# Three more unread 128-column products at the start, in place of 33 small ones

## The chip, the cores and the metric

One core of a Trainium2 chip runs the whole kernel. The metric is the device time of one execution in microseconds (us); lower is better. The kernel before takes 313.28 us (median of 3 runs, 313.25 to 313.35). TensorE is called PE here (its weight loads PEld), VectorE DVE, ScalarE ACT, GpSimd POOL, and SyncE, which issues the data transfers, SP.

## What is computed

The inputs are q, k and v (4 batches, 4 heads, 1088 positions, 32 features), two small projections S1 and S2 (8 by 32), and the weights of a gated layer. With `phi(x)` the outer product of `x @ S1.T` and `x @ S2.T` (64 features), the first part is linear attention:

```python
kv = sum over s of phi(k)[s] v[s];  z = sum over s of phi(k)[s]
x  = (phi(q) @ kv) / (phi(q) @ z + 1e-06)          # heads side by side: (4, 1088, 128)
```

The second part, per batch:

```python
h = relu(x @ w_in); u, v = h[..., :512], h[..., 512:]
v_n = (v - mean(v)) / sqrt(var(v) + 1e-06)
v_s = w_spatial @ v_n + b_spatial[:, None]
out = (u * v_s) @ w_out
```

## The kernel before

The long products are made in three passes over operands that are split into a high and a low half (`wTh`/`wTl`/`wl`, `vh`/`vl`, `xh`/`xl`, lines 1172 to 1183 and 1417 for the positions, 606 to 608 for the others). Work goes batch by batch. A batch begins with its attention: `project` (line 781) makes the two projections of keys or queries, ACT copies one of them (`ka`, line 786), DVE multiplies them out into the features (`kp`, line 788), and `part` (line 818) sums features times values into `kv`. Line 818 is a burst of very short PE instructions: products of 32 features by 33 columns, four of them side by side, 72 products for a batch. PE makes a product of full 32-bit floats in two passes, and each pass is one weight load and one matmul in the trace, so the 72 products are 144 loads and 144 matmuls. In batch 0 the burst comes in three parts (`kv0:1` to `kv0:3`, with 24 products each), in the other batches in one (`kv1`, `kv2`, `kv3`).

The order of the work is written out by hand: `SEQ` lists every operation by name and engine (`kab00:1@PE` is the first projection of the keys of batch 0), and each engine runs its own entries in that order. `Order.schedule` replays the list with planned costs to choose buffers and the order in which the instructions are written down. It also puts unread filler products (`Fill`, line 638, 128 columns) before a PE operation where its plan leaves PE room, up to the time `FILL_TO`. In batch 0 PE's list is: the warm-up `wps:1` to `wps:7`, `kab00`, `kab01`, `kab02`, `kv0:1`, `qab00`, `kv0:2`, `kv0:3`, `tq00`, `tq01` (transposes of the query features, line 863), `qab01`, `qab02`, `nd00` (line 877), and so on to `xt0` (line 891).

The warm-up is work that nobody reads. DVE fills a tile `z9` (lines 622 and 623); `wps:1` is the function `small`, which makes 33 products of 32 columns, spread over the four quarters of the array, and `wps:2` to `wps:7` are one product of 128 by 128 columns each (line 633). All write the same bank. The first real work of PE, `kab00`, needs the projection weights `sk`, which DVE prepares, and the first tile of keys, which SP loads.

Of the kernel before, what the change touches and what calls it, by code (L numbers as in the profile page):

```python
# [35 lines left out]

EXP_LO = 2.0 ** -15
EXP_HI = 122879.9921875
N_SMALL, N_WARM = 33, 6


PS_BUFS = {"po": 3, "sp": 2, "pu": 1, "sd": 2}
# [17 lines left out]
AFTER_W = (7.0, 13.0, 13.0)  # L60

SEQ = """
s_raw:1@SP z9:1@DVE z9:2@DVE wi_raw1:1@SP eps:1@ACT v92:1@POOL wps:1@PE v90:1@POOL kt00:1@SP v91:1@POOL wz:1@POOL kt01:1@SP wps:2@PE kt02:1@SP
wps:3@PE v93:1@POOL v00:1@SP wps:4@PE sk:1@DVE mask_sb:1@SP wps:5@PE sk:2@DVE sk:3@DVE qt00:1@SP wps:6@PE sk:4@DVE sk:5@DVE wps:7@PE v01:1@SP sk:6@DVE
sk:7@DVE b32:1@SP wi_x1:1@DVE v02:1@SP wi_x1:2@DVE kab00:1@PE ident_sb:1@SP wi_x1:3@DVE qt01:1@SP kab01:1@PE ka00:1@ACT qt02:1@SP kp00:1@DVE
ka01:1@ACT eps:2@DVE kp01:1@DVE kab02:1@PE kv0:1@PE ka02:1@ACT wi_raw0:1@SP qab00:1@PE kp02:1@DVE wt30:1@SP qa00:1@ACT wt10:1@SP qp00:1@DVE kv0:2@PE
wt80:1@SP kv0:3@PE wi_x1:4@DVE tq00:1@PE tq01:1@PE kd0:1@DVE qpT00:1@ACT wi_x1:5@DVE qab01:1@PE qpT01:1@ACT wi_x1:6@DVE qab02:1@PE qa01:1@ACT
nd00:1@PE qp01:1@DVE wi_x1:7@POOL qa02:1@ACT wi_x0:1@ACT wt01:1@SP qp02:1@DVE wt11:1@SP tq10:1@PE wt50:1@SP tq11:1@PE rec0:1@DVE qpT10:1@ACT wt00:1@SP
rec0:2@DVE tq20:1@PE wih:1@ACT x320:1@DVE wt20:1@SP wi_x0:2@DVE bh:1@ACT qpT11:1@ACT xt0:1@PE wt21:1@SP wil:1@DVE tq21:1@PE xh0:1@ACT wTl:10@SP
nd01:1@PE wi_x0:3@DVE wt40:1@SP xl0:1@DVE wTh:10@ACT wt31:1@SP wTh:9@ACT wi_x0:4@DVE pv000:1@PE wt41:1@SP qpT20:1@ACT rec1:1@DVE qpT21:1@ACT wt51:1@SP  # L70
# [247 lines left out]
class Order:  # L318
# [12 lines left out]
    def op(self, eng, cost, fn, r=(), w=(), kb=0, alts=(), sh=False, after=0.0, f4=False, name=None):  # L331
        o = Op()
        o.n, o.eng, o.fn, o.kb, o.f4 = len(self.ops), eng, fn, kb, f4
        o.alts = ((eng, cost, fn), *alts)
        name = name or next(((x[0] if isinstance(x, tuple) else x).name for x in w), "out")
        self.named[name] = self.named.get(name, 0) + 1
        o.name = f"{name}:{self.named[name]}"
        o.sh, o.after, o.behind = sh, after * 1e3, None
        deps = {}
        r, w = ([(t, key) for t0, key in (x if isinstance(x, tuple) else (x, None) for x in xs) for t in (t0.tiles if isinstance(t0, Whole) else [t0])] for xs in (r, w))  # L340

        def split(x):
            return x if isinstance(x, tuple) else (x, None)

        def touching(table, t, key):
            for (t2, k2), v in table.get(t, {}).items():
                if key is None or k2 is None or k2 == key:
                    yield (t2, k2), v

        for x in r:  # L350
            t, key = split(x)
            for _, d in touching(self.last_w, t, key):
                deps[d] = True
        for x in w:
            t, key = split(x)
            for _, d in touching(self.last_w, t, key):
                deps[d] = True
            for _, ds in touching(self.readers, t, key):
                for d in ds:
                    deps[d] = True  # L360
        for x in r:
            t, key = split(x)
            self.readers.setdefault(t, {}).setdefault((t, key), []).append(o)
        for x in w:
            t, key = split(x)
            for k, _ in list(touching(self.last_w, t, key)):
                if key is None or k[1] == key:
                    del self.last_w[t][k]
            for k, _ in list(touching(self.readers, t, key)):
                if key is None or k[1] == key:  # L370
                    del self.readers[t][k]
            self.last_w.setdefault(t, {})[t, key] = o
        deps.pop(o, None)
        o.deps, o.succ = list(deps), []
        for d in o.deps:
            d.succ.append(o)
        o.tiles = list(dict.fromkeys(split(x)[0] for x in (*r, *w)))
        o.first = []
        for t in o.tiles:
            if t.tag is not None:  # L380
                o.first.append(t)
                t.users.append(o)
        self.ops.append(o)
        return o
# [148 lines left out]
def tile_kernel(ctx: ExitStack, tc: tile.TileContext, kT, qT, vA, sks, idn, msk, wT, w_in, w_out, bsp, out):  # L533
# [6 lines left out]
    nc = tc.nc  # L540
# [59 lines left out]
    op, tl = k.op, k.tile  # L600

    def bank(tag, name):
        return tl(tag, name, [P, 512])
# [17 lines left out]
    z9 = tl("u", "z9", [P, P])  # L621
# [1 line left out]
    op("DVE", 165, lambda: nc.vector.memset(z9[64:66], 1.0), w=[z9])  # L623

    wps = bank("sd", "wps")
    def small():
        for i in range(N_SMALL):
            q = 32 * (i % 4)
            nc.tensor.matmul(wps[q:q + 32, :32], z9[:, q:q + 32], z9[:, :32], start=True, stop=True, tile_position=(0, q))

    op("PE", 1100, f4=True, fn=small, r=[z9], w=[wps])
    for i in range(N_WARM):
        op("PE", 420, f4=True, fn=lambda: nc.tensor.matmul(wps[:, :P], z9.ap, z9.ap, start=True, stop=True), r=[z9], w=[wps])

# [7 lines left out]
    eps = tl(None, "eps", [P, 2])  # L642
# [57 lines left out]
    sk = tl(None, "sk", [P, 2 * NSK])  # L700
    s_raw = tl("pl", "s_raw", [P, 384])
# [8 lines left out]
    kd0 = tl("u", "kd0", [P, 2, 2, D + 1])  # L710
# [288 lines left out]
    def hidden_v(b, st, g):  # L999
# [39 lines left out]
        def small(out, in0, scalar, in1, op0, op1, r, w):  # L1039
            op("DVE", 163, lambda: v.scalar_tensor_tensor(out=out(), in0=in0(), scalar=scalar, in1=in1(), op0=op0, op1=op1), r=r, w=w, sh=True)  # L1040

        small(lambda: t1.ap, lambda: mv[:, :, 1], LN_EPS, lambda: rs.ap, ALU.add, ALU.mult, [rs, mv], [t1])
        small(lambda: t1.ap, lambda: t1.ap, -0.5, lambda: rs.ap, ALU.mult, ALU.mult, [rs], [t1])
        small(lambda: rs.ap, lambda: t1.ap, 1.5, lambda: rs.ap, ALU.add, ALU.mult, [t1], [rs])

# [592 lines left out]
```

## Time and profile before

| what | value |
|---|---|
| median of 3 runs | 313.28 us |
| the profiled execution, its own time | 313.46 us |
| its span on the core | 311.7 us |
| instructions in the span | 6906 |
| PE busy | 305.7 us (98%) |
| DVE, ACT, POOL busy | 221.0, 180.0, 94.3 us |

The span runs from the first to the last instruction of the program; 1.76 us of the profiled execution lie around it. All numbers of rows below come from that one execution, with times from the start of the span. A PE that is busy is not PE at its peak, since matmuls are pipelined and their ends are modelled. "issue" as the cause of a wait means that the engine waited for no semaphore that the profile shows.

### The profile page before, as it was taken

To read this page: it belongs to the slowest core of one execution; us is meant where nothing else is said; L and a number is where in the kernel's file an instruction comes from. 1 tells how busy PE (TensorE), PEld (TensorE's weight loads), DVE (VectorE), ACT (ScalarE), POOL (GpSimd) and SP (SyncE) were. 2 spreads that over 40 slices of the span, in tenths; PEclk is the share of its full clock that TensorE was granted. 3 is DMA by queue.
4 is the path that set the end of the run, shared out by engine and by line. 5 is a ranking of instruction groups with operands and counts; after the bars stand their busy time and mean duration, and the time that the engine had idled before them with its cause. 6 is when DMAs were issued, how large, how long until landed. Compare 5 with 4: busy or idle time off the path is not lost.

```text
span 311.7 us, 6906 instructions
## 1 busy us (share of the span) xinstructions
PE 305.7 (98%) x2588; PEld 294.7 (95%) x2588; DVE 221.0 (71%) x549; ACT 180.0 (58%) x428; POOL 94.3 (30%) x124
## 2 busy tenths in 40 slices
PE   7899999999999999999999999999999999999995
PEld 7788999999999999999999999999999999999995
DVE  6899977636666855473694478898976767978572
ACT  2499974525765553567564776897346345654430
POOL 2145015243311046652113654510110312152400
PEclk9999999999999999999999999999999999999999
DMA  7974147573300055710334864223000170410002
GB/s 243 311 219 161 28 139 207 180 210 103 86 1 23 3 155 158 214 52 0 124 90 141 294 214 117 87 64 84 25 0 2 35 299 0 144 47 0 2 0 72
DMA packets 22989, 33.78 MB, mean 108 GB/s; under 512 B 2988, under 2 KB 21420, under 8 KB 22956
## 3 DMA queue, kind: packets, MB, share of 16 engines
q1 hardware_dynamic: 22812, 33.21, 33.7%
q8 instruction: 20, 0.33, 0.5%
q10 hardware_dynamic: 144, 0.13, 0.1%
q14 instruction: 13, 0.11, 0.1%
HBM read 26.79 MB, written 6.54 MB: 107 GB/s over the span
## 4 chain that ended last, share of the span: by engine, by line
PE 96%; DVE 2%; issue 1%; ACT 0%; DVEq 0%; ACTq 0%
PE sp L1172 15%; PE sp L1174 13%; PE sp L1181 13%; PE sd L1417 9%; PE sp L1417 7%; PE sd L606 4%; PE sd L607 4%; PE sd L608 4%; PE pu L606 3%; PE po L606 3%; PE pu L608 3%; PE pu L607 3%; PE po L607 2%; PE po L608 2%; PE sp L1183 2%; PE sd L781 2%
## 5 line engine op out<-in xcount | busy, mean ns | idle before, releaser
L1172 PE MATMUL sp<-wTh,vh 128*128 128x332 f32 (+1 forms) x286 | 93.7, 329 | 0.0
L1174 PE MATMUL sp<-wTh,vl 128*128 128x332 f32 (+1 forms) x240 | 78.7, 328 | 0.0
L1172 PEld LDWEIGHTS sp<-wTh,vh 128*128 128x128 f32 x286 | 53.7, 188 | 0.5
L1174 PEld LDWEIGHTS sp<-wTh,vl 128*128 128x128 f32 x240 | 45.1, 188 | 0.2
L1181 PE MATMUL sp<-wl,vh 128*128 128x332 f32 x128 | 39.7, 310 | 0.0
L1181 PE MATMUL sp<-wTl,vh 128*128 128x424 f32 x112 | 38.0, 348 | 0.0
L614 DVE TENSOR_TENSOR g<-u,g 128x332 fp32r<-128x332 f32 (+1 forms) x41 | 24.6, 600 | 11.9 <-ACT g L693 6.2
L1165 ACT ACTIVATE u<-pu 128x332 f32<-128x332 f32 (+1 forms) x44 | 20.6, 467 | 19.5 <-PE pu L608 11.7
L1209 DVE TENSOR_TENSOR u<-sp,u 128x332 f32<-128x332 f32 (+1 forms) x43 | 22.3, 521 | 11.7 <-PE sp L1183 10.8
L1013 DVE BATCH_NORM_STATS2 st<-vt 128x6 f32<-128x512 f32 x36 | 24.3, 685 | 8.3 <-ACT vt L1011 8.1
L617 POOL TENSOR_TENSOR r<-pl,r 128x384 fp32r<-128x384 f32 (+1 forms) x18 | 17.8, 996 | 32.0 <-ACT r L693 13.7
L1011 ACT ACTIVATE vt<-sd 128x512 f32<-128x512 f32 x36 | 21.1, 601 | 11.0 <-PE sd L608 10.6
L693 ACT CAST g<-u 128x332 fp32r<-128x332 f32 (+1 forms) x41 | 20.0, 489 | 8.6 <-DVE u L1209 3.5
L950 POOL TENSOR_TENSOR pl<-pl,pl 128x384 f32<-128x384 f32 (+1 forms) x18 | 17.9, 1001 | 21.7 <-DMA pl<-qd 7.6
L1181 PEld LDWEIGHTS sp<-wl,vh 128*128 128x128 f32 x128 | 24.0, 188 | 0.0
L1085 ACT CAST vh<-vt 128x384 fp32r<-128x384 f32 x44 | 21.5, 509 | 1.8 <-DVE vt L1049 1.1
L1181 PEld LDWEIGHTS sp<-wTl,vh 128*128 128x128 f32 x112 | 21.0, 188 | 0.1
L1087 POOL TENSOR_TENSOR vl<-vt,vh 128x384 fp32r<-128x384 f32 (+1 forms) x16 | 14.6, 914 | 21.1 <-ACT vh L1085 16.9
L1052 ACT ACTIVATE vt<-vt,sm,sm 128x512 f32<-128x512 f32 x18 | 14.4, 814 | 3.5 <-DVE sm L1040 3.5
L986 DVE STREAM_TRANSPOSE sd<-c 128x384 f32<-128x384 f32 (+1 forms) x9 | 5.1, 568 | 15.9 <-ACT c L983 15.8
L606 PE MATMUL pu<-xh,wih 128*128 128x332 f32 (+1 forms) x48 | 16.0, 334 | 0.0
L1087 DVE TENSOR_TENSOR vl<-vt,vh 128x384 fp32r<-128x384 f32 (+1 forms) x28 | 14.3, 515 | 2.1 <-ACT vh L1085 2.0
(317 smaller groups left out, 805.4 us busy)
## 6 DMA issues: line engine op xcount, KB each, us to landing
pl<-in_wT SPq DMA_DIRECT2D x34, 166.0 KB
v<-in_vA SPq DMA_DIRECT2D x12, 198.0 KB
kt<-in_kT SPq DMA_DIRECT2D x12, 192.0 KB
pl<-qd SPq DMA_DIRECT2D x12, 192.0 KB
pl<-qd SPq DMA_DIRECT2D x24, 96.0 KB
vd<-vt SPq DMA_DIRECT2D x3, 768.0 KB
vt<-vd SPq DMA_DIRECT2D x3, 768.0 KB
c<-in_qT SPq DMA_DIRECT2D x9, 192.0 KB
```

The source lines that it names most:

```text
L606: nc.tensor.matmul(o, ah, bh, start=start, stop=False)
L607: nc.tensor.matmul(o, ah, bl, start=False, stop=False)
L608: nc.tensor.matmul(o, al, bh, start=False, stop=stop)
L614: return lambda: nc.vector.tensor_tensor(out=o(), in0=a(), in1=bb(), op=ALU.subtract)
L1013: op("DVE", 690, lambda stats=stats, t=t: nc.vector.bn_stats(out=stats.ap, in_=vt[:, t]), r=[(vt, t)], w=[stats])
L1085: op("ACT", c_act(384), lambda: nc.scalar.copy(out=vh[:, kk:kk + 3], in_=x()), r=vr, w=[(vh, g)])
L1087: return lambda: eng.tensor_tensor(out=vl[:, kk:kk + n], in0=x()[:, :n], in1=vh[:, kk:kk + n].bitcast(F32), op=ALU.subtract)
L1172: nc.tensor.matmul(sp[:, :cw], vh[:, kt], wTh[:, kt, cs], start=(kt == begin), stop=False)
L1174: nc.tensor.matmul(sp[:, :cw], vl[:, kt], wTh[:, kt, cs], start=False, stop=False)
L1181: nc.tensor.matmul(sp[:, :cw], vh[:, kt], w_lo(kt, c), start=False, stop=False)
L1209: op("DVE", c_dve(cw), lambda: nc.vector.tensor_tensor(out=u.ap, in0=sp[:, :cw], in1=u.ap, op=ALU.mult), r=[sp], w=[u])
L1417: nc.tensor.matmul(x[:, :cw], p, q, start=i == 0 and n == 0, stop=end and i == 3 and n == 2)
```

## The change

`small` and its operation go, and the warm-up gets nine products of 128 columns in place of six. The list of the work is changed to match: PE has `wps:1` to `wps:9`, and the entries of the other engines keep their order. Apart from line breaks, `SEQ` differs in nothing else.

```diff
-N_SMALL, N_WARM = 33, 6
+N_WARM = 9
...
-s_raw:1@SP z9:1@DVE z9:2@DVE wi_raw1:1@SP eps:1@ACT v92:1@POOL wps:1@PE v90:1@POOL kt00:1@SP v91:1@POOL wz:1@POOL kt01:1@SP wps:2@PE kt02:1@SP
-wps:3@PE v93:1@POOL v00:1@SP wps:4@PE sk:1@DVE mask_sb:1@SP wps:5@PE sk:2@DVE sk:3@DVE qt00:1@SP wps:6@PE sk:4@DVE sk:5@DVE wps:7@PE v01:1@SP sk:6@DVE
...
+s_raw:1@SP z9:1@DVE z9:2@DVE wi_raw1:1@SP eps:1@ACT v92:1@POOL wps:1@PE v90:1@POOL kt00:1@SP wps:2@PE v91:1@POOL wz:1@POOL wps:3@PE kt01:1@SP wps:4@PE
+kt02:1@SP v93:1@POOL wps:5@PE v00:1@SP wps:6@PE sk:1@DVE mask_sb:1@SP sk:2@DVE wps:7@PE sk:3@DVE qt00:1@SP sk:4@DVE wps:8@PE sk:5@DVE v01:1@SP
+sk:6@DVE wps:9@PE sk:7@DVE b32:1@SP wi_x1:1@DVE v02:1@SP wi_x1:2@DVE kab00:1@PE ident_sb:1@SP wi_x1:3@DVE qt01:1@SP kab01:1@PE ka00:1@ACT qt02:1@SP
...
     wps = bank("sd", "wps")
-    def small():
-        for i in range(N_SMALL):
-            q = 32 * (i % 4)
-            nc.tensor.matmul(wps[q:q + 32, :32], z9[:, q:q + 32], z9[:, :32], start=True, stop=True, tile_position=(0, q))
-
-    op("PE", 1100, f4=True, fn=small, r=[z9], w=[wps])
     for i in range(N_WARM):
         op("PE", 420, f4=True, fn=lambda: nc.tensor.matmul(wps[:, :P], z9.ap, z9.ap, start=True, stop=True), r=[z9], w=[wps])
```

## Rows read from the trace of the kernel before

**Rows 1.** The page, part 1: busy us, share, instructions of each engine.
```profile
PE 305.7 (98%) x2588; PEld 294.7 (95%) x2588; DVE 221.0 (71%) x549; ACT 180.0 (58%) x428; POOL 94.3 (30%) x124
```
**Rows 2.** Waits of PE, whole run: us in total, times, longest.
```profile
PE pu L818 <- issue: 0.9, 1, 0.9
PE sp L891 <- DVE c L884: 0.3, 1, 0.3
```
**Rows 3.** Timeline of PE, 0 to 12 us: start, us, instruction, count, idle before.
```profile
1.30 1.17 PE L629 MATMUL sd<-u 128*32 128x32 f32 x66 [1.30 <-DVE u L623]
2.40 2.93 PE L633 MATMUL sd<-u 128*128 128x128 f32 x12
8.88 0.60 PE L818 MATMUL pu<-v,kp 128*32 128x33 f32 x44
10.35 0.88 PE L818 MATMUL pu<-v,kp 128*32 128x33 f32 x52 [0.87 <-issue]
11.16 0.87 PE L863 MATMUL po<-u,kp 128*128 128x128 f32 x6
...
11.96 0.92 PE L781 MATMUL sd<-sk,c 128*64 128x64 f32 x24
```
**Rows 4.** Timeline of PEld, 4 to 6 us.
```profile
5.40 0.72 PEld L781 LDWEIGHTS sd<-sk,kt 128*64 128x64 f32 x18 [0.37 <-DVE vt L673]
```
**Rows 5.** Line 633: ns min/median/max of one, first and last start.
```profile
L633 PE MATMUL sd<-u x12: 421/421/582, 2.4 to 4.9; 128*128 128x128 f32 x12
```
**Rows 6.** The page, part 3: DMA packets, MB, share of 16 engines.
```profile
q8 instruction: 20, 0.33, 0.5%
```
**Rows 7.** Windows: stretch, us, busy (xcount) PE, PEld, DVE, ACT, POOL, PEclk, DMA, GB/s.
```profile
0.00:6.04 6.04, 4.64 (x96) 4.31 (x98) 3.29 (x12) 1.49 (x3) 2.21 (x9) 1.00 0.65 210
0.00:8.13 8.13, 6.48 (x154) 5.83 (x156) 5.25 (x15) 2.16 (x5) 2.21 (x9) 1.00 0.76 248
0.00:10.34 10.34, 7.83 (x222) 6.95 (x222) 7.29 (x18) 2.44 (x6) 2.21 (x9) 1.00 0.81 259
0.00:11.96 11.96, 9.44 (x280) 8.27 (x280) 8.42 (x21) 2.66 (x7) 2.21 (x9) 1.00 0.82 250
10.34:65.53 55.19, 54.87 (x424) 50.88 (x424) 45.31 (x106) 38.68 (x92) 18.72 (x18) 1.00 0.57 174
275.90:295.11 19.21, 19.21 (x130) 19.12 (x129) 13.69 (x34) 8.38 (x23) 9.54 (x15) 1.00 0.05 17
```
**Rows 8.** DMA view, windows 8.02:8.04, 13.91:13.93, 67.06:67.08, 118.32:118.34: packets, MB, share.
```profile
q8 instruction: 1, 0.02, 290.1%
...
q8 instruction: 1, 0.02, 274.7%
...
q8 instruction: 1, 0.02, 299.4%
...
q8 instruction: 1, 0.02, 343.1%
```
**Rows 9.** Timeline of PE, 64.9 to 67.3 and 115.3 to 117.4 us.
```profile
65.53 1.53 PE L818 MATMUL sd<-v,kp 128*32 128x33 f32 x144
67.00 0.42 PE L1172 MATMUL sp<-wTh,vh 128*128 128x332 f32 x1
...
115.57 1.68 PE L818 MATMUL sd<-v,kp 128*32 128x33 f32 x144
```
**Rows 10.** Timeline of DVE, 7 to 16 us.
```profile
7.19 3.03 DVE L788 TENSOR_TENSOR kp<-ka,sd 128x768 f32<-128x768 f32 x3
...
11.27 0.30 DVE L842 TENSOR_TENSOR u<-pu,mask_sb 128x132 f32<-128x132 f32 x1 [0.45 <-PE pu L818]
12.85 1.82 DVE L788 TENSOR_TENSOR kp<-ka,sd 128x768 f32<-128x768 f32 x2 [0.23 <-ACT ka L786]
```
**Rows 11.** Lines of PE, 5.4 to 9.4 us: busy us, mean ns of one.
```profile
L781 PE MATMUL sd<-sk,kt 128*64 128x64 f32 x36 | 1.6, 229 | 0.3 <-DVE eps L650 0.2
L638 PE MATMUL po<-u 128*128 128x128 f32 x4 | 0.7, 300 | 0.0
```

More of the change, by code (lines that the diff above doesn't have):

```diff
@@ L62 @@
 SEQ = """
-s_raw:1@SP z9:1@DVE z9:2@DVE wi_raw1:1@SP eps:1@ACT v92:1@POOL wps:1@PE v90:1@POOL kt00:1@SP v91:1@POOL wz:1@POOL kt01:1@SP wps:2@PE kt02:1@SP
-wps:3@PE v93:1@POOL v00:1@SP wps:4@PE sk:1@DVE mask_sb:1@SP wps:5@PE sk:2@DVE sk:3@DVE qt00:1@SP wps:6@PE sk:4@DVE sk:5@DVE wps:7@PE v01:1@SP sk:6@DVE
-sk:7@DVE b32:1@SP wi_x1:1@DVE v02:1@SP wi_x1:2@DVE kab00:1@PE ident_sb:1@SP wi_x1:3@DVE qt01:1@SP kab01:1@PE ka00:1@ACT qt02:1@SP kp00:1@DVE
-ka01:1@ACT eps:2@DVE kp01:1@DVE kab02:1@PE kv0:1@PE ka02:1@ACT wi_raw0:1@SP qab00:1@PE kp02:1@DVE wt30:1@SP qa00:1@ACT wt10:1@SP qp00:1@DVE kv0:2@PE
-wt80:1@SP kv0:3@PE wi_x1:4@DVE tq00:1@PE tq01:1@PE kd0:1@DVE qpT00:1@ACT wi_x1:5@DVE qab01:1@PE qpT01:1@ACT wi_x1:6@DVE qab02:1@PE qa01:1@ACT
+s_raw:1@SP z9:1@DVE z9:2@DVE wi_raw1:1@SP eps:1@ACT v92:1@POOL wps:1@PE v90:1@POOL kt00:1@SP wps:2@PE v91:1@POOL wz:1@POOL wps:3@PE kt01:1@SP wps:4@PE
+kt02:1@SP v93:1@POOL wps:5@PE v00:1@SP wps:6@PE sk:1@DVE mask_sb:1@SP sk:2@DVE wps:7@PE sk:3@DVE qt00:1@SP sk:4@DVE wps:8@PE sk:5@DVE v01:1@SP
+sk:6@DVE wps:9@PE sk:7@DVE b32:1@SP wi_x1:1@DVE v02:1@SP wi_x1:2@DVE kab00:1@PE ident_sb:1@SP wi_x1:3@DVE qt01:1@SP kab01:1@PE ka00:1@ACT qt02:1@SP
+kp00:1@DVE ka01:1@ACT eps:2@DVE kp01:1@DVE kab02:1@PE kv0:1@PE ka02:1@ACT wi_raw0:1@SP qab00:1@PE kp02:1@DVE wt30:1@SP qa00:1@ACT wt10:1@SP qp00:1@DVE
+kv0:2@PE wt80:1@SP kv0:3@PE wi_x1:4@DVE tq00:1@PE tq01:1@PE kd0:1@DVE qpT00:1@ACT wi_x1:5@DVE qab01:1@PE qpT01:1@ACT wi_x1:6@DVE qab02:1@PE qa01:1@ACT
 nd00:1@PE qp01:1@DVE wi_x1:7@POOL qa02:1@ACT wi_x0:1@ACT wt01:1@SP qp02:1@DVE wt11:1@SP tq10:1@PE wt50:1@SP tq11:1@PE rec0:1@DVE qpT10:1@ACT wt00:1@SP
```

## Prediction

> **What bounds the kernel now.** I read the page's busy times first, then PE's waits over the whole run, then the first 12 us in the timeline, and last where the program's own code is loaded. PE is busy for 98% of the span [rows 1], and after 16 us it has no wait that the list of waits would show [rows 2]. So PE's work in line is the bound: a stall of PE anywhere is paid in full, and off the path lies only what ends before PE needs it, which happens in the first 16 us alone. The reader should see in PE's waits that by far the longest after the start is 0.87 us ahead of 10.35 us, and that its cause is "issue": no semaphore was missing [rows 2, 3]. It also falls into the middle of an operation. `kv0:2` is 48 passes; 44 run at 8.88 us, and the last 4 run with the next operation's 48 at 10.35 us [rows 3]. Nothing between the 44th and the 45th pass is waited for in the program. What is missing is the instructions.
>
> How code arrives can be read from the small queue q8. It moves 20 packets, 0.33 MB, so 16 KB each [rows 6]; PE has 2588 matmuls and 2588 loads [rows 1], or some 260 for each packet. Between the last two packets (275.90 and 295.11 us) lie 130 matmuls and 129 loads [rows 7]. So I take q8 as PE's code, in blocks of 256 instructions. The count at the stall fits: 222 loads and 222 matmuls precede it [rows 7], and with a few wait instructions and the program's opening that can be two blocks, 512. Call that place P. One packet comes before it, at 8.02 us [rows 8]. I read it so: two blocks are there at the start; entering the second, at P-256, makes the core ask for the third; the third is not there when PE reaches P. P-256 is about instruction 190 of the rows and lies at 6.04 us (96 matmuls, 98 loads) [rows 7]. From asking to packet it took 2.0 us, from packet to PE going on 2.3 us, 4.3 in all.
>
> [...]
>
> **The change, part by part.** *Removed:* 66 loads and 66 matmuls at line 629 (33 products, two passes each) [rows 3]. *Added:* 3 products; six now give 12 passes [rows 3], so 6 loads and 6 matmuls more. PE's program is 132 - 12 = 120 instructions shorter ahead of everything real. *Moved:* no entry of another engine, no transfer and no wait; in the planner the warm-up's end goes from 1300 + 1100 + 6 x 420 = 4920 ns to 1300 + 9 x 420 = 5080, which makes room for no further filler.
>
> *The warm-up itself: nothing.* The 12 passes start from 2.4 to 4.9 us [rows 5], at 0.21 us for each of the later ones (0.42 us long, two in flight). Eighteen from 1.30 us put the last start at 1.30 + 2.5 + 6 x 0.21 = 5.1 us, its columns through by 5.3. `kab00` begins at 5.40 after 0.37 us of idle time [rows 4]: it waits for the keys, and this wait hides the 0.2 us. Without that cover it would cost 0.2.
>
> *The block boundaries: two effects.* Every boundary now falls 120 instructions later in the work.
>
> First, the early stall moves. P now lies 120 instructions further: between 10.34 and 11.96 us are 58 loads and 58 matmuls [rows 7] and a few waits, so P is at the first loads of `qab01` (11.96 us [rows 3]). It is asked for at old P-136, about instruction 310 of the rows, at 8.13 us [rows 7]. With the same 2.0 and 2.3 us it is there at 12.4. Without stall PE could be there sooner than now: `tq00` needs the query features that DVE ends at 10.2 us (7.19 + 3.03 [rows 10]), then 0.8 us of transposes [rows 3], so 11.0. It will therefore wait there, 1.4 us in place of 0.87, and `qab01` starts at 12.4 instead of 11.96: +0.45. That goes on: DVE at 12.85 us waits for the copy of `qab01` [rows 10], and from there the chain runs to PE's wait of 0.3 us for DVE at line 891 [rows 2]. Bounds: if code is there by 11.0, DVE loses its 0.45 us wait and the 0.23 us one [rows 10], a gain of 0.7. If the request takes the 3.6 us of the second packet (10.35 to 13.91 [rows 3, 8]), code comes at 8.1 + 3.6 + 2.3 = 14.0: +2.0. I take +0.45, the same request measured once under the same load.
>
> Second, a new stall. The old boundaries after P come every 256. From 10.34 to 65.53 us are 424 + 424 instructions [rows 7] and about a dozen waits, 860; P+768 lies 92 before the burst `kv1` at 65.53 us, and the next, P+1024, within it at 66.3, followed by long passes. So at present PE has 7 us for one block and some 11 for the next. The new boundary P+888 falls about 28 instructions into the burst, at 65.7 us, and the next one 256 later. The burst is 144 loads and 144 matmuls [rows 9]: the second boundary falls at its last handful, near 66.85 us. So a block asked for at 65.7 is needed after 1.2 us. The packet of the old boundary in this burst came at 67.06 [rows 8], 0.8 us after 66.3. By that the new packet comes at 66.5; code follows after 0.9 us (the packet's own length: 290.1% of 16 engines' 0.02 us [rows 8]) to 2.3 (the early case), so at 67.4 to 68.8. The stall is 0.55 to 1.95; I take 1.2, the middle. Bounds: the sequencer may ask up to 0.4 us earlier, since long passes precede the burst, giving nearly nothing; a request of 1.6 us gives 2.7. That is the longest that I can read in a burst: an old boundary lies within `kv2`, 115.57 to 117.2 us [rows 9], by the count of blocks at 116.7, and its packet came at 118.33 [rows 8]. No cover: PE is the bound here.
>
> Elsewhere a block lasts several us (the bursts of batches 2 and 3 get no second boundary, by the same count), which hides the fetch.
>
> Sum: 0.45 + 1.2 = +1.65. The profiled execution is 313.46 us (311.7 of span and 1.76 around it), 0.18 above the median, and would be 315.1; against the median 313.28 the forecast is **314.9 us**.
>
> **The rivals.**
> *Faster (0.09).* The early stall goes and the new one is hidden. It has one place, the request at 8.13 us: it would find the data queue emptier than the one at 6.04, and the third block would be there by 11.0. For it: nothing yet lags from an earlier packet. Against it: DMA is as full as before, 0.81 to 0.82 over both stretches [rows 7]. Price -0.7, so 312.6; it decides if the code takes under 2.9 us and PE asks for the `kv1` block before 65 us.
>
> *No change that can be measured (0.19).* Either code is really mostly hidden and the 0.87 us was something else, or a gain of 0.5 early meets a stall of 0.6 to 1.0 in `kv1`. 313.3 to 313.8. Against the first: the stall stands in the middle of an operation and at a multiple of the block.
>
> *The clock (0.07).* The small products could be what lifts PE to its higher level. [...] Against it: 18 full passes keep PE as busy as the old mix. [...]
>
> **How the numbers follow.** The forecast, a new stall in `kv1` with an early stall about as long as now or longer, has 0.65. Its own range is 313.9 to 316.4 (early -0.3 to +1.0 and late 0.6 to 2.2). The range goes down to the case without measurable change and up to the slow ends: 313.1 to 316.4. A difference under 0.2% (0.63 us) can hardly be told from none here. Slower: 0.65 + 0.07 = 0.72; same 0.19; faster 0.09.
>
> **What would show it.** In the profile after: 120 loads and matmuls fewer (2528 of each), `kab00` still at 5.40 us; no idle time in the midst of `kv0:2`; PE idle for "issue" before about the first passes of `qab01`, until 12.4 us; a q8 packet near 10.1 and one near 66.5 us; and a new PE wait for "issue" of about 1.2 us at the last passes of line 818 around 67 us. Were PE idle in neither place, or `kab00` late, the prediction would be wrong.

## The result and the profile after

The kernel after takes 316.86 us (median of 6 runs, 315.35 to 319.49); the kernel before took 313.39 us in the same job (6 runs, 313.25 to 314.90). The ratio is 1.011, with a 95% interval of 1.0062 to 1.0159. (Ratios leave out runs over 1.5% above the fastest of their kernel: below, three of `after_again` and one each of `after_pad30` and `wide_small_later`.) The forecast was 314.9 us, 313.1 to 316.4: the direction is right, the time lies 2 us above it and outside the range.

The six runs differ in the clock that was granted to PE, as a mean over the run: 315.35 and 315.95 us at 1.0; 316.14, 317.58 and 317.93 at 0.994 to 0.995; 319.49 at 0.989. The profiled execution is the 315.35 us one, with a span of 313.6 us (311.7 before). Its page has, in parts 1 and 3 [rows 1, 6]:

```profile
PE 305.6 (97%) x2528; PEld 294.8 (94%) x2528; DVE 219.5 (70%) x549; ACT 180.1 (57%) x428; POOL 94.4 (30%) x124
...
q8 instruction: 20, 0.33, 0.5%
```

PE's waits over the whole run (us in total, times, longest), which answer to [rows 2]. The code stall in batch 0's `kv0` is gone, and two others are there. Line numbers behind `small` are 6 lower than before, so 812 is the old 818 and 775 the old 781:

```profile
PE sd L812 <- issue: 1.0, 1, 1.0
PE sd L775 <- ACT c L861: 0.9, 1, 0.9
PE sd L775 <- DMA kt<-in_kT: 0.9, 2, 0.6
PE sp L885 <- DVE c L878: 0.3, 1, 0.3
```

The timeline of PE, 0 to 19 us (start, length, instruction, count, idle before and what ended it), which answers to [rows 3]:

```profile
1.31 3.84 PE L627 MATMUL sd<-u 128*128 128x128 f32 x18 [1.31 <-DVE u L623]
5.75 0.57 PE L775 MATMUL sd<-sk,kt 128*64 128x64 f32 x12 [0.61 <-DMA kt<-in_kT]
...
9.31 1.10 PE L812 MATMUL pu<-v,kp 128*32 128x33 f32 x96
10.71 0.87 PE L857 MATMUL po<-u,kp 128*128 128x128 f32 x6 [0.29 <-DVE kp L782]
12.48 0.92 PE L775 MATMUL sd<-sk,c 128*64 128x64 f32 x24 [0.90 <-ACT c L861]
13.33 1.55 PE L871 MATMUL sp<-u,c 128*128 128x66 f32 x12
14.72 1.15 PE L857 MATMUL po<-u,kp 128*128 128x128 f32 x9
```

And the same view from 65.5 to 70 us, beside [rows 9]:

```profile
66.04 1.49 PE L812 MATMUL sd<-v,kp 128*32 128x33 f32 x141
68.53 0.25 PE L812 MATMUL sd<-v,kp 128*32 128x33 f32 x3 [1.00 <-issue]
68.71 0.42 PE L1166 MATMUL sp<-wTh,vh 128*128 128x332 f32 x1
```

The reader is to see the two forecast places. The 96 passes of `kv0:2` and `kv0:3` run through, and PE stands still ahead of `qab01` until 12.48 us. The profile names ACT's copy as its releaser, but ACT's two copies ran from 11.29 to 12.15 us, `qab01` of the kernel before started in the midst of them (11.96, copies 11.74 to 12.60 us), and the same wait in two later executions of this kernel is listed as "issue". In `kv1` 141 passes run, and the last 3 come 1.00 us later. The q8 packets ahead of the two places came at 9.65 and at 66.23 us (DMA view, windows 9.64 to 9.66 and 66.22 to 66.25); PE went on 2.8 and 2.3 us after them.

```profile
q8 instruction: 1, 0.02, 448.8%
...
q8 instruction: 1, 0.02, 194.4%
```

Where the 1.9 us of this execution went: the burst `kv1` starts at 66.04 in place of 65.53 us (+0.51), and the long passes behind it at 68.71 in place of 67.00 (+1.71, so 1.20 more). The forecast for the two was 0.45 and 1.2. The last 0.2 us come later and are not followed here. What this doesn't explain is how the other runs come to be up to 4 us longer than this one.

### The profile page after: what moved, and what is told of

Its sections match the earlier page's. It is cut to its first block, busy times and chain, and to the rows that moved or that the text cites. A ratio compares the mean times of both kernels' runs of the same rounds, so it can differ in the third digit from the quotient of the medians.

```text
span 313.6 us, 6786 instructions
## 1 busy us (share of the span) xinstructions
PE 305.6 (97%) x2528; PEld 294.8 (94%) x2528; DVE 219.5 (70%) x549; ACT 180.1 (57%) x428; POOL 94.4 (30%) x124
## 4 chain that ended last, share of the span: by engine, by line
PE 95%; DVE 1%; DMA 1%; issue 1%; SPq 0%; ACT 0%; DVEq 0%; ACTq 0%
PE sp L1166 15%; PE sp L1168 13%; PE sp L1175 13%; PE sd L1411 9%; PE sp L1411 7%; PE sd L606 4%; PE sd L608 4%; PE sd L607 4%; PE pu L606 3%; PE po L606 3%; PE pu L608 2%; PE pu L607 2%; PE po L607 2%; PE po L608 2%; PE sp L1177 2%; PE sd L775 2%
```

## The experiments

**The same kernel again.** To find what differs between its runs, the kernel after was timed again, and three more single executions of it were profiled (`after_look1` to `after_look3`).

> The changed kernel once more, unaltered. Theory A (code blocks): PE idle for 'issue' about 1.0 us within the last passes of kv1 near 67 us and until about 12.4 us before qab01; the executions whose granted clock is full take 315.3 to 316.0 us. Theory B (the warm-up): the stalls are the small part, and what lifts the median to 316.9 is that PE's clock is at its lower level for a while in most executions, since the small products are gone; granted clock under 1.0 in about 4 of 6 executions. Both may hold; the trace of an execution with a granted clock under 1.0 would show when it was low.

315.98 us (11 runs, 314.17 to 319.22) against 313.91 (16 runs), ratio 1.0055 [1.0035, 1.0075]. Eight runs at a granted clock of 0.999 or 1.0 take 314.17 to 316.74 us, with a median of 315.6; three at 0.989 take 318.98 to 319.22. So at full clock the change costs 1.7 us here, and a second cost comes with the clock. The three single executions took 315.61 (clock 1.0), 317.35 (0.993) and 317.31 us (0.994).

> The changed kernel, unaltered, one look, to meet an execution in which the granted clock is under 1.0 (7 of 17 so far) and to see when PE's clock fell. Theory C1 (stalls): it falls after the stall before qab01 or after the one in kv1 (12 or 68 us). Theory C2 (warm-up): it falls in the first 12 us, after the waits for the keys near 5.4 and 6.4 us, or rises late.

The second of them, `after_look2`, timeline of PE from 9 to 20 us:

```profile
9.21 1.10 PE L812 MATMUL pu<-v,kp 128*32 128x33 f32 x96
10.61 0.87 PE L857 MATMUL po<-u,kp 128*128 128x128 f32 x6 [0.30 <-DVE kp L782]
13.07 0.92 PE L775 MATMUL sd<-sk,c 128*64 128x64 f32 x24 [1.58 <-issue]
13.91 2.32 PE L871 MATMUL sp<-u,c 128*128 128x66 f32 x12
16.03 2.07 PE L857 MATMUL po<-u,kp 128*128 128x128 f32 x9
```

and windows of it (stretch, length, busy time and count of PE, PEld, DVE, ACT and POOL, granted clock, DMA share, GB/s):

```profile
12.00:14.00 2.00, 0.93 (x25) 0.86 (x24) 0.48 (x2) 0.29 (x2) 1.27 (x1) 1.00 0.71 232
15.00:17.00 2.00, 2.00 (x11) 2.00 (x11) 1.42 (x4) 0.10 (x2) 0.00 (x0) 0.50 1.07 395
```

The early stall is 1.58 us here, and after it the granted clock is down, to 0.50 from 15 to 17 us. The 12 passes of line 871 take 2.32 us in place of 1.55, the 9 of line 857 2.07 in place of 1.15. `kv1` starts at 67.75 us, 2.2 later than before: 1.1 from the stall (13.07 against 11.96) and 1.1 from the slower passes. `after_look3` has the same, with 1.71 us of stall. `after_look1` (1.3 us of stall) and the profiled run of `after_again` (0.46 us) keep the full clock.

**The stall in `kv1` alone.** The kernel before, with 34 unread small products (136 instructions) ahead of `tq21`, late enough to leave batch 0's code where it was.

```diff
-                def turn(pr=pr, tp=tp, qp=qp):
+                def turn(pr=pr, tp=tp, qp=qp, g=g):
+                    for i in range(34 if (g, pr) == (2, 1) else 0):
+                        c = 32 * (i % 4)
+                        nc.tensor.matmul(tp[c:c + 32, 480:512], ident[:, c:c + 32], ident[:, :32], start=True, stop=True, tile_position=(0, c))
```

> The kernel before with 34 unread small products (136 PE instructions, about 0.7 us) ahead of the transposes tq21 near 18 us; 136 more is the same place in a block of 256 as 120 fewer. Theory A: the early part as before (0.87 us in kv0:2), and the stall of 1.0 us in the last passes of kv1 as in the changed kernel; 313.3 + 0.7 + 1.0 to 1.2 = 315.0 to 315.2 at full clock. If that stall brings the clock down, granted clock under 1.0 in several executions and a median of 316 or more. Theory B: 313.3 + 0.7 = 314.0, full clock.

315.77 us (6 runs), ratio 1.0064 [1.004, 1.0089], the granted clock full in all six. Timeline of PE around 68 us:

```profile
66.31 1.42 PE L818 MATMUL sd<-v,kp 128*32 128x33 f32 x134
68.67 0.25 PE L818 MATMUL sd<-v,kp 128*32 128x33 f32 x3 [0.94 <-issue]
```

(The view starts inside the burst, which is 141 passes from 66.24 us and then 3.) The place of the block boundary makes this stall: nothing of the warm-up was touched. It doesn't bring the clock down in these six runs. The early stall, expected at 0.87 us as before, is nearly gone in this execution, though its code lies as before: the second tile of keys came 0.6 us late, the packet came at 7.64 in place of 8.03 us, and the 96 passes take 1.30 us, against 1.10 where nothing stops them. So the early stall of the kernel before is no fixed number either.

**Padding the changed kernel.** The same edit in the kernel after, with 15 products (60 instructions) and with 30 (120), which puts the later boundaries half way and all the way back.

> The changed kernel with 15 unread small products (60 PE instructions, about 0.3 us by the 10.6 ns of a pass in the burst) ahead of the transposes tq21 near 18 us. Theory A: the boundary in kv1 moves 60 instructions earlier in the work, its block is asked for some 2 us sooner; no stall at 67 us, the early one before qab01 stays; 1.0 less the 0.3 = 0.7 us faster than the changed kernel where the clock is full (about 314.6 to 315.2). If the stall in kv1 also brings the clock down, the granted clock is full in nearly all executions and the median near 315. Theory B: clock under 1.0 as often as in the changed kernel, median 316 to 317.

> The changed kernel with 30 unread small products (120 PE instructions, about 0.6 us) ahead of the transposes tq21 near 18 us: from there on the blocks lie as in the kernel before. Theory A: the early stall before qab01 stays as in the changed kernel, with a clock that falls after it in 3 to 5 of 10 executions; no stall in kv1, kv2 or kv3. Over the kernel before: 0.6 for the products, 0.2 to 1.4 for the early stall, so 0.8 to 2.0 us at full clock and some 1.7 to 3.4 more where the clock falls.

With 15: 316.47 us (6 runs, one at clock 0.988), 1.0101 [1.0067, 1.0136], above the 314.6 to 315.2 expected. Its `kv1` runs its 144 passes through, the early stall stays (`qab01` at 12.56 us), and one that I had not forecast stands behind `kv2`; timeline from 116 us:

```profile
116.68 1.53 PE L812 MATMUL sd<-v,kp 128*32 128x33 f32 x144
118.14 0.42 PE L1169 MATMUL sp<-wTh,vh 128*128 128x332 f32 x1
119.48 0.31 PE L1171 MATMUL sp<-wTh,vl 128*128 128x332 f32 x1 [0.92 <-issue]
```

With 30: 315.3 us (12 runs, two at 0.989), 1.0056 [1.0034, 1.0079]; no wait for "issue" is left in its list, and the early one is

```profile
12.53 0.92 PE L775 MATMUL sd<-sk,c 128*64 128x64 f32 x24 [0.63 <-ACT c L864]
```

`after_pad30` keeps the early stall alone, and two of its 12 runs have the lower clock; `before_pad34` has the late one, and none of its 6 does. These counts are too small to tell the two stalls apart, and the runs at the lower clock here have no trace.

**What brings the clock down: the missing small products, or the stall?** Two kernels cross the two. In the first the warm-up is the changed one (nine wide products), and 32 small ones stand in place of the two fillers behind `kab01`, so that the boundaries lie as before. In the second the warm-up is the old one, with its small products, and 36 more stand in place of the fillers, so that more boundaries fall early.

```diff
-        nc.tensor.matmul(homes[tag, slot][:, :P], z9.ap, z9.ap, start=True, stop=True)
+        for i in range(16):     # 18 in the second
+            q = 32 * (i % 4)
+            nc.tensor.matmul(homes[tag, slot][q:q + 32, :32], z9[:, q:q + 32], z9[:, :32], start=True, stop=True, tile_position=(0, q))
```

> The nine products of 128 columns as in the changed kernel, and 32 small ones (128 instructions) in place of the two fillers after kab01: from there on PE's blocks lie as in the kernel before. Theory A: stall in kv0:2 as before or up to 0.5 us longer (that boundary's block is asked for near 6.6 us), none before qab01, none in kv1: 313.3 to 314.5 at full clock, within 0.6 us of the kernel before. If low clock comes from the stalls (C1), full clock in all executions; if from the warm-up without small products at its start (C2), granted clock under 0.996 in about 4 of 10 executions and a higher median.

> The kernel before, its warm-up with 33 small products unaltered, and 36 more small ones (144 instructions) in place of the two fillers after kab01. Theory A: the block asked for in kab01 is now needed in kv0:1 near 8.5 us and comes at 10.35, the next one is asked for there and needed at qab01, where it comes near 14.4: two stalls of about 2 us each, a third of 0.5 to 1.2 us in kv1; 3 to 5 us slower than before. C1 (a long stall brings the clock down): granted clock under 0.996 in most executions, though the small products stand at the start. C2 (without small products the clock is not held): full clock, 3 us slower at most.

The first: 314.72 us, 8 runs, seven of them at full clock (314.06 to 315.38); ratio 1.0032 [1.0013, 1.0051] (313.3 to 314.5 was expected). The eighth took 319.89 us at clock 0.984, and it is the one with a profile. Timeline and windows of it:

```profile
9.14 0.60 PE L814 MATMUL pu<-v,kp 128*32 128x33 f32 x44
12.63 1.02 PE L814 MATMUL pu<-v,kp 128*32 128x33 f32 x52 [2.89 <-issue]
```
```profile
9.00:11.00 2.00, 0.74 (x52) 0.56 (x48) 1.89 (x3) 0.24 (x1) 0.00 (x0) 1.00 0.78 242
12.00:15.00 3.00, 2.37 (x58) 2.02 (x58) 1.26 (x3) 0.48 (x1) 0.00 (x0) 0.50 0.93 303
```

The second: 320.01 us, 4 runs, 1.0206 [1.017, 1.0242], all four at 0.989 to 0.995, with small products in the warm-up and behind it. PE's waits, and a window behind the stall of 2.4 us, which ends at 15.81 us:

```profile
PE sd L783 <- issue: 2.4, 1, 2.4
...
PE pu L820 <- issue: 1.2, 1, 1.2
PE sd L820 <- issue: 0.6, 1, 0.6
```
```profile
18.00:20.00 2.00, 2.00 (x12) 2.00 (x12) 1.74 (x5) 0.66 (x2) 0.00 (x0) 0.50 0.03 10
```

With wide products alone in the warm-up (the small ones come later, at 6.9 us) the clock is kept in seven of eight; the kernel after, which has no small products at all, kept it in 10 of 17 runs; and small products don't keep it where the stalls are long. The rival that the small products hold the clock falls. In each of the five traces in which the clock fell while PE still had work, it fell inside a stall of code of 1.6 us or more, or within 2 us of its end.

**Moving the boundaries on purpose.** If their place decides, another number of warm-up instructions could beat both kernels. Four were tried: 56, 28 and 8 instructions more than before, and 32 fewer (the warm-up's entries in `SEQ`, and its planned cost where needed, follow, so that no filler comes or goes).

```diff
-N_SMALL, N_WARM = 33, 6
+N_SMALL, N_WARM = 48, 5     # blocks_free
+N_SMALL, N_WARM = 41, 5     # blocks_28_earlier
+N_SMALL, N_WARM = 35, 6     # blocks_8_earlier
+N_SMALL, N_WARM = 24, 7     # blocks_32_later
```

> 48 small products and 5 of 128 columns in place of 33 and 6: the warm-up lasts as long, and PE's program is 56 instructions longer ahead of everything real. Theory A: the boundaries fall 56 instructions earlier in the work, none has its block asked for under 5 us before it is needed; no stall in kv0:2 and none in kv1, 0.5 to 0.9 us faster than before (312.5 to 312.9). Theory B: the same kind of warm-up as before, so the same time (313.3). Both: full granted clock.

> 41 small products and 5 of 128 columns in place of 33 and 6: PE's blocks begin 28 instructions earlier in the work. Theory A: the block of the early stall is asked for at kab00 (5.35 us) and not in kab01 (5.9), so the stall in kv0:2 ends 0.5 us sooner, about 9.85 in place of 10.35; no stall in kv1, kv2 or kv3, whose boundaries stay outside the critical places. 0.3 to 0.5 us faster than before, full clock. Rival B (the shape of the warm-up counts, not the blocks): the same time as before within 0.1 us.

> 24 small products and 7 of 128 columns: PE's blocks begin 32 instructions later. Theory A: the block is asked for in kab02 (about 7.3 us) and needed in kv0:3, so it comes some 4 to 4.5 us later: a stall of 1 to 2 us in kv0:3 that ends near 11.5 us; no stall in the later bursts. 0.5 to 1.0 us slower than before at full clock, and in some executions the clock falls after the stall, for 1.7 us more. Rival B: as before within 0.2 us, since the warm-up lasts as long and has small products.

> The kernel before with 6 wide products ahead of kv0 and two fillers of 35 and 34 small products in place of its own, so that PE's program is 8 instructions longer ahead of kv0 and every boundary of 256 falls 8 instructions earlier in the work. By the theory (a packet comes 2.2 to 2.8 us before PE goes on, the place of the boundary decides what it stops): the stall in kv0:2 ends near 9.9 us in place of 10.35, the next block costs 0.1 us or nothing, kv1 to kv3 show no stall of code; 312.9 to 313.6 us, 0 to 0.4 us faster than before. By the rival that any shift of the boundaries costs because a request made earlier meets a fuller DMA queue: the packet after the first stall is late and the time is 0.5 to 2 us above before.

(That text describes the edit wrongly: the kernel has 35 small and 6 wide products in the warm-up, and the fillers of the kernel before. The 8 instructions are right.)

*blocks_free*: 317.47 us (6 runs, 315.2 to 318.47; two at clock 0.993 and 0.994), 1.0106 [1.0074, 1.0138], a miss by 5 us. In the profiled execution, the fastest of the six (315.2 us), the stall in `kv0` is gone, as forecast, but another stands in `kv3`, which I had not counted, and the second tile of keys is late. What makes the other five longer is not shown.

```profile
7.15 0.57 PE L781 MATMUL sd<-sk,kt 128*64 128x64 f32 x12 [1.22 <-DMA kt<-in_kT]
...
166.36 0.22 PE L818 MATMUL sd<-v,kp 128*32 128x33 f32 x1 [1.11 <-issue]
```

*blocks_28_earlier*: 315.14 us (12 runs), 1.0039 [1.0023, 1.0055], a miss too. The stall in `kv0` ends at 9.98 us (9.85 forecast), but the next block, by the count asked for about then, has its packet at 14.59 us only, and PE goes on at 17.07, 2.5 us after it (the row names an ACT copy). The longest wait of this execution is another, 1.3 us for DVE near 262 us, so that the code explains a part of the miss alone:

```profile
9.98 0.80 PE L818 MATMUL pu<-v,kp 128*32 128x33 f32 x66 [0.60 <-issue]
...
17.07 1.22 PE L877 MATMUL sp<-u,c 128*128 128x66 f32 x10 [0.80 <-ACT xh L895]
```
```profile
PE sp L1417 <- DVE u L1209: 1.3, 1, 1.3
```

*blocks_32_later*: 315.85 us (6 runs), 1.0065 [1.0042, 1.0087], above the 0.5 to 1.0 us expected, since beside the forecast stall in `kv0` (until 11.60 us, 11.5 forecast) `kv2` has one:

```profile
11.60 0.53 PE L818 MATMUL pu<-v,kp 128*32 128x33 f32 x37 [1.63 <-issue]
...
118.98 0.32 PE L818 MATMUL sd<-v,kp 128*32 128x33 f32 x13 [1.43 <-issue]
```

*blocks_8_earlier*: 313.77 us (12 runs), 1.0015 [0.9994, 1.0035]: no difference from before that this can show. The early stall shrinks to 0.3 us inside the burst (96 passes in 1.44 us against 1.10 in the kernel after), and no code is late afterwards. But this execution waits 0.9 us for DVE near 260 us, and the gain of half a microsecond isn't seen in the time. The same wait comes with 0.2 to 1.3 us in six other traces, with either warm-up, and is not listed in the rest; whether it belongs to these edits is open.

```profile
9.02 1.44 PE L818 MATMUL pu<-v,kp 128*32 128x33 f32 x96
```

So of the places tried none beats the kernel before.

**Why the same stall has several lengths.** In seven executions with the changed warm-up (`after`, `after_again`, `after_look1` to `after_look3` and the two kernels below) the packet for `qab01` starts between 0.3 us (9.65, burst at 9.31) and 1.8 us (11.35, burst at 9.57) after the burst `kv0:2`, a fixed place of the program, and PE goes on 2.2 to 2.8 us after the packet. So it is the packet that comes late, not the code behind it. To see whether data ahead of it make it wait, two unread copies of 512 KB, DRAM to DRAM, were put near the late stall: first just ahead of the load `kt20`, then some 2 us sooner, in batch 1's loads.

```diff
+                            for m in range(2):
+                                t = dr.tile([P, 1024], U32, name=f"more{m}")
+                                nc.sync.dma_start(out=t, in_=w_in[:, m * 512:m * 512 + 512].bitcast(U32))
```

> The changed kernel with two unread copies of 512 KB each, DRAM to DRAM, put on SyncE just ahead of the load of kt20, near 65 us. If the time that a code packet waits is set by the data queued before it (the theory): the packet for the last passes of kv1, which comes 0 to 0.7 us after its request in the kernels without the copies, comes 1 to 3 us after it, and the stall at the last passes of kv1 grows from 0.5 to 1.2 us to 2 to 4 us, so 317.5 to 319.5 us, more if the granted clock falls after it. If the code's way is its own (the rival): the stall stays at 0.5 to 1.2 us, and the time at that of the changed kernel, 315 to 317 us, unless kt20 itself lands late and key blocks show waits on it.

> As after_more_data, but the two unread 512 KB copies are put on SyncE some 2 us sooner, ahead of the second half of a load of batch 1 near 63.6 us. There, issued from 65.5 us, their data came from 67 us, behind the code packet at 66.42; the next packet came 3.3 us after PE went on at 68.83, against 1.3 us in the changed kernel (69.83 after 68.53). Issued near 63.6 the data come from about 65 us, ahead of the request of some 66.2. If the packet waits behind data (the theory): packet at 67 to 69 us, stall at the last passes of kv1 of 1.5 to 4 us in place of 0.5 to 1.2, so 316.5 to 319.5 us. If the code's way is its own (the rival): packet at 66.2 to 66.9, stall 0.5 to 1.2 us, 314.5 to 317 us.

Late: 315.59 us (6 runs, all at 0.998 to 1.0), 1.0073 [1.0048, 1.0098]. The copies were issued from 65.5 us, and their data came behind the packet of 66.42 us. The stall is as before:

```profile
66.80 1.49 PE L820 MATMUL sd<-v,kp 128*32 128x33 f32 x141
68.83 0.25 PE L820 MATMUL sd<-v,kp 128*32 128x33 f32 x3 [0.54 <-issue]
```

By the letter that is the rival's result, but the copies did not stand where the theory wants them. Sooner: 321.0 and 324.3 us (clock 0.989 and 0.983) against 314.21, 1.026 [1.0125, 1.0394]. The copies were issued at 64.21 us. Its waits, its timeline, the packet in the DMA view's window 69.63 to 69.68, and three windows around the stall:

```profile
PE sd L812 <- issue: 3.0, 1, 3.0
PE sd L775 <- issue: 1.9, 1, 1.9
```
```profile
67.45 1.51 PE L812 MATMUL sd<-v,kp 128*32 128x33 f32 x141
71.98 0.32 PE L812 MATMUL sd<-v,kp 128*32 128x33 f32 x3 [3.02 <-issue]
```
```profile
q8 instruction: 1, 0.02, 115.1%
```
```profile
70.00:71.00 1.00, 0.00 (x0) 0.00 (x0) 0.00 (x0) 0.00 (x0) 0.00 (x0) 1.00 0.98 294
71.00:72.00 1.00, 0.02 (x2) 0.02 (x1) 0.00 (x0) 0.00 (x0) 0.00 (x0) 0.56 1.04 340
72.00:74.00 2.00, 2.00 (x9) 1.93 (x9) 1.19 (x6) 0.78 (x2) 1.00 (x1) 0.50 0.83 219
```

The packet comes 2.2 us after the burst's start (69.65 against 67.45), in place of 0.2 us after it in the profiled execution of the kernel after (66.23 against 66.04) and 0.3 to 0.6 us ahead of it in its four other executions and with the late copies; PE goes on 2.3 us after the packet, as elsewhere. The stall is 3.0 us, and now the clock falls to 0.50 at this place, where the 0.9 us stall of `before_pad34` left it alone. So here data queued ahead made the code late, and the stall that they lengthened was followed by the lower clock. Only two runs were timed, and one has a trace. Its packet for `qab01`, long before the copies, was the latest of the seven too, so this could be an execution in which all code comes late; against that, `after_look2` and `after_look3`, with early packets almost as late (1.6 and 1.7 us behind the burst's start), have their `kv1` packets 0.3 and 0.5 us ahead of the burst.

## Why the prediction was right in its mechanism and wrong in its size

*Blocks of 256, 120 instructions later.* Right. The stall left `kv0:2` and came up ahead of `qab01` and at the last passes of `kv1`, as forecast, and other numbers of instructions moved it as the count says: in batch 0, counted from the start of `kv0:2`, from behind the 44th pass to behind the 30th with 28 instructions more and behind the 59th with 32 fewer; in `kv1` behind the 141st both with 120 fewer and with 136 more, which are 256 apart; in `kv2` from behind the burst and one long pass, 290 instructions (60 fewer), to behind 131 passes, 262 instructions (32 fewer). I had not counted `kv2` and `kv3` out. At `qab01` and in `kv1` the code was not there in time: PE stood still for 0.90 and 1.00 us in the profiled execution. What no run shows is a request: how many blocks are there at the start, when the next is asked for, and the 2.0 us from asking to packet are the author's estimate from one stall. By it PE was to go on in batch 0 at 9.85 us with 28 instructions more, at 11.5 with 32 fewer and at 12.4 with 120 fewer; it went on at 9.98, at 11.60 and, over seven executions, at 12.09 to 13.73 us. In `kv1` the estimate failed (below).

*The warm-up itself costs nothing.* Right in its own terms: 18 passes end at 5.15 us, and the keys landed later (`kab00` at 5.75 us). That start was forecast at 5.40, and a late `kab00` was named as a sign of being wrong; the row names the transfer of the keys as its cause (0.61 us of idle time). The prediction read this wait as the keys' before too, where its row names DVE's line 673, which makes a tile that `kab00` doesn't read. `kab00` starts at 5.44 to 5.99 us in ten executions with the new warm-up and at 5.35 to 5.46 in six of seven with the old one (5.84 in the seventh), so the first tile of keys does land later; why isn't shown. By the first burst, `kv0:1`, the two groups no longer differ (7.84 to 8.57 us against 7.82 to 8.79).

*The stall in `kv1`, +1.2 us.* Right: 1.00 us of idle time and 1.20 us in the chain in the profiled execution; 0.35 to 0.7 us of idle time in the four other executions of the kernel. The mean of the five, 0.6 us, is near the lower end of its range. Two errors offset each other here: the prediction has the block asked for 28 instructions into the burst, but in those four the packet came 0.3 to 0.6 us before the burst began, and PE went on 2.3 to 2.5 us behind the packet, not 0.9 to 2.3.

*The early stall, +0.45 us.* This is the step that failed. Its place was right, and in the profiled execution its end was, too (12.48 us against 12.4), but that was luck: `kab00` was 0.35 us late, the packet came at 9.65 in place of 10.1 us, and PE went on 2.8 us after it in place of 2.3. It was priced as one number, "the same request measured once under the same load". Over the seven executions PE goes on at 12.09 to 13.73 us, so +0.1 to +1.8 and +0.8 in the mean, since the packet starts 0.3 to 1.8 us behind the burst. The bound of +2.0 in the text held that; the range took +1.0 of it. And what follows a long stall was put at nothing: behind the longer of these stalls the granted clock is 0.50 for some microseconds (15 to 17 us in `after_look2`, 15 to 18 in `after_look3`), 1.1 us more in `after_look2`. A mean clock under 0.996 is listed for 7 of 17 timed runs of the kernel after, against 1 of 73 of the kernel before whose clock was listed. Those 7 runs have no trace; that the fall stands behind the early stall in them too is inferred from `after_look2` and `after_look3`.

At full clock the kernel after takes 315.6 us in its median in `after_again`, 1.7 above before: the forecast sum, though not its terms. In the three full-clock traces the delay up to `kv1` and the one in it are 0.51 and 1.20, 0.41 and 0.56, and 1.04 and 0.56 us. In the first job two of six runs are at full clock, 2.0 and 2.6 us above before; the other four, 2.8 to 6.1 us above it, carry the median out of the range. (The prediction's own ends, -0.3 + 0.6 and 1.0 + 2.2, give 313.6 and 316.5, not 313.9 and 316.4; the measured time lies outside either way.)

*The rivals.* "The clock" was right that the clock would cost time, and wrong about how: it put the loss down to the missing small products at the start, but in the profiled execution the first 12 passes on the keys take 0.57 us at 5.75 us, as 12 such passes do at 8.81 us, and in `after_again` they take 0.70, 0.13 more. What cost time is a fall later on, behind a stall (to 0.50 after 1.58 us in `after_look2`). (The listed granted clock does not tell slower passes at the start: it is 1.00 from 0 to 6 us, while the 18 warm-up passes take 3.84 us, 0.21 each, near the 0.23 of the 9 of the same shape that take 2.07 us at 0.50; at full clock 9 take 1.15.) "No change" and "Faster" fell with the two stalls.

*What stays open.* Not every long stall is followed by the lower clock: 1.63 us in `blocks_32_later` and 1.9 us early in `after_data_sooner` were not. How often it comes differs between jobs (four of six, three of eleven, and none of six in `after_more_data`, whose batch 0 is the same); the later jobs ran on different chips, and nothing here separates the chip from chance. And why the packet's delay differs between executions of one program was not tried; data queued ahead made it in one execution at `kv1`, and are not shown to have made it in batch 0.

## What to carry to other kernels

Removing or adding instructions that cost nothing shifted every later block of PE's code here: with 120 fewer the stall left the 44th pass of `kv0:2`, and others stood ahead of `qab01` and behind the 141st pass of `kv1`. In a kernel that one engine bounds, count in such blocks, 256 here, through all the dense bursts (all of them, not the next one), and look at each boundary for what has to be fetched while short instructions run (0.35 to 1.4 us of standstill in `kv1`, `kv2` and `kv3`) and what data are queued then (3.0 us in the execution with 1 MB ahead). Where a stall may vary in length, time the kernel with its granted clock listed for each run: the profiled execution may be the one that got off lightly (here 315.35 us, where others of its six took up to 319.49).

## What the runs showed of the hardware

- From the q8 packet to PE going on it took 2.2 to 2.8 us at the stalls quoted here, early or late, and 2.3 us with 1 MB queued ahead; what varies is when the packet comes. For `kv1` it came between 0.6 us before and 0.2 us after the burst's start in six executions, and 2.2 us after it in the one with 1 MB queued ahead.
- A burst of 144 short passes, loads and matmuls, is 288 instructions in 1.5 us and so longer than the 256 after which the place of a stall came again (120 fewer and 136 more, `kv1`). Where two boundaries fell into it, or the second just behind it, PE stood still for 0.35 to 1.4 us (`kv1`, `kv2` and `kv3` above; 3.0 us with the data queued ahead).
- The stalls of code before a fall of the granted clock were 1.6, 1.7, 2.4, 2.9 and 3.0 us; those up to 1.43 us were never followed by one in a trace, and two of 1.63 and 1.9 us were not either.
